# Two mixture-of-experts layers behind a Fourier transform: another order of the 26 products and other PSUM banks

## The chip, the cores and the metric

The kernel runs on one core of a Trainium2 chip. The metric is the device time of one execution in microseconds (us). The kernel before took 10217.74 us (median of 3 runs, 10211.21 to 10218.54).

## The reference

```python
X = np.fft.fft(np.fft.fft(x, axis=1), axis=2)      # x: 8 x 3072 x 256
x = X.real.reshape(24576, 256)
...                                                 # first layer: each row goes to the best one of 8 experts
logits = x @ w_gate;  P = np.exp(logits - logits.max())
for _ in range(8):                                  # Sinkhorn balancing
    P /= P.sum(1, keepdims=True) + 1e-09
    P /= P.sum(0, keepdims=True) + 1e-09
    P *= N / E
for e in range(8):                                  # second layer: every row through every expert
    h = np.maximum(x @ w1[e], 0.0)                  # 256 -> 1024
    out += P[:, e:e + 1] * (h @ w2[e])              # 1024 -> 256
```

All is float32. The change lies in the second layer.

## The kernel before

The first 1850 us hold the transform, the routing and the first layer. The second layer (class `Second`, line 778) fills the rest. It takes the 24576 rows in 24 blocks of 1024, and each block through the 8 experts: 192 rounds, a round being one block `b` and one expert `e`.

In a round the first matrix product `x @ w1[e]` is not done as 32 block products but by a fast scheme with 26: the rows' and the weights' blocks are added and subtracted beforehand, and sums of the 26 products give the 16 hidden blocks of 128 features by 512 columns. The table `STEPS` (line 722) is that scheme and also its schedule. One entry is one **step**, numbered 0 to 25 here. It holds: the PSUM bank (0 to 3) into which the product goes; 1 if the bank starts a new sum, 0 if the product is added to what stands there; the signs of the weight blocks; the sums of row blocks to be formed; which row block is used; a list of operations; and the banks that are free for other use at this step.

The operations of a step, in the loop at line 1105:

- `c k`: ACT copies the bank's running sum to an SBUF tile `v` number k (line 1120, named c18 and so on below).
- `a k`: DVE forms tile k from two others or from the bank (-1) and a tile (line 1125; the tile is called `v` where it is kept, `z` where it goes straight into a hidden block).
- `h o`: ACT takes the positive part of hidden block o, rounded to the matmul's type (line 1061).
- `l o`: DVE forms the rest that the rounding lost (line 1067).
- `m o`: TensorE multiplies hidden block o by w2, 12 matmuls into another four banks (line 1032). A last number 1 means that the block of the round before is meant.

A step's own product is 6 matmuls of 256 columns (line 1114), so a round has 26 x 6 + 16 x 12 = 348. TensorE's order is that of the program. The other engines each work through a queue that a scheduler has laid out when the kernel is built. A product into a bank may start only when every operation that reads the bank's sum so far is done, whether the product adds to that sum or starts a new one. So what counts is how long a bank rests between the last product in it and the next.

During a block's rounds e=6 and e=7 the next block's rows are prepared (`prepare`, line 952): in e=6 TensorE transposes them in four groups of four (`pb`), each group in a bank that the current step lists as free (`bank`, line 947; asked for at steps 0, 4, 8, ... , one group at a time, the first free bank of the list), and ACT copies each to `xb`. Then POOL forms the sums `xt` (line 968), ACT casts each of the 26 operands to `xs` (line 490, "cast"), and POOL forms the rest that the cast lost (line 491). Each `xs` has one buffer, so the cast for step m has to wait for step m of round e=7. In block 0 the Sinkhorn balancing runs beside rounds 0 to 4.

Of the kernel before, what the change touches and what calls it, by code (L numbers as in the profile page):

```python
# [525 lines left out]
class First:  # L526
# [99 lines left out]
    def run(self, second):  # L626
# [93 lines left out]


STEPS = [
# [52 lines left out]
]  # L775


class Second:
# [6 lines left out]
    def weights(self, raw, pool):  # L785
# [18 lines left out]
        for e in range(E):  # L804
            yield
            yield
            for pc in range(NP // 2):
                o = pool.tile([128, 2, 2, 2, 128], F32R, name="qo", tag="qo")
                for n in range(2):
                    a = STEPS[2 * pc + n][2]  # L810
                    v = [(c, r1[:, i % 2, :, i // 2, :]) for i, c in enumerate(a) if c]
# [93 lines left out]
    def run(self, ones, r):  # L905
        nc, tc = self.nc, self.tc
        from contextlib import ExitStack
        with ExitStack() as ctx:
            pool = lambda name, bufs, **k: ctx.enter_context(tc.tile_pool(name=name, bufs=bufs, **k))
            one, xp = pool("n1", 1), pool("nx", 1)  # L910
            ring, ring2 = pool("nw", NW), pool("nw2", NW2)
            hp, vp, zp, hsp = pool("nh", 8), pool("nv", 11), pool("nz", 3), pool("ns", 2)
            ph, py = pool("nph", 1, space=PSUM), pool("npy", 1, space=PSUM)
            ctx.enter_context(tc.manual_schedule(engines={mybir.EngineType.PE}))

# [3 lines left out]
            for k in (1, 0):  # L919
                for s in STEPS:  # L920
                    for o in s[5]:
# [30 lines left out]
            def prepare(r, xs, fast):  # L952
                eng = nc.vector if fast else nc.gpsimd
                blk = {}
                for k in range(2):
                    for h in range(2):
# [6 lines left out]
                        if not fast:  # L963
                            yield
                for m, s in enumerate(STEPS):
                    for o, x, y, c in s[3]:
# [82 lines left out]

            outs = [o[1] for k in (1, 0) for s in STEPS for o in s[5] if o[0] == "m" and o[2] == 1 - k]  # L1050
            cnt, firstj = [0] * 4, None
# [32 lines left out]
            def advance(n):  # L1084
                nonlocal ahead
                for _ in range(n - ahead):
                    next(prep, None)
                ahead = max(ahead, n)

            late_x = None  # L1090
            for u, (b, e) in enumerate(rounds):
# [8 lines left out]
                if (b, e) == (0, HELD):  # L1100
# [3 lines left out]
                    accp[0] = pool("na", 1)  # L1104
                for m, (bk, new, _, _, _, ops, idle) in enumerate(STEPS):
                    if b == e == 0:
# [37 lines left out]
                    if e == 0 and b > 0:  # L1144
                        advance(8 + min(NP, int((m + 24) / 1.5) + 1))
            for s in STEPS:
                for o in s[5]:
# [70 lines left out]
```

## Time and profile before

| | |
|---|---|
| median of 3 runs | 10217.74 us |
| the profiled execution | 10225.79 us |
| its span, first to last instruction | 10224.0 us |
| mean granted TensorE clock | 0.976 |
| busy: PE, DVE, ACT, POOL | 96%, 66%, 44%, 19% |
| second layer: first product, last matmul starts | 1856.1 us, 10211.4 us |

In the profile PE is TensorE's matmuls and PEld its weight loads; DVE, ACT, POOL and SP are the other engines. The end of a matmul in a row is modelled and overlaps the next one's start, so waits of TensorE are read from starts. In steady work matmuls of 256 columns start 0.12 us apart.

### The profile page before, as it was taken

The numbers are of one execution on the slowest core, as the hardware profiler recorded it, in microseconds if no ns is written. First come the engines' busy times: TensorE is split into PE (matmuls) and PEld (weight loads), VectorE is DVE, ScalarE is ACT, GpSimd is POOL, SyncE is SP. The second block draws the span as 40 slices with busy tenths as digits, with TensorE's granted clock in tenths as the row PEclk, the third lists the DMA queues.
The fourth block names the chain that finished last, engine by engine and source line by source line (L and its number), as shares of the span: only waits on it lengthen the run. The fifth ranks groups of instructions, "written<-read, shape, count | busy, mean of one in ns | idle before, by whom it ended". The sixth has DMA issues, their size and how long they took to land.

```text
span 10224.0 us, 194490 instructions
## 1 busy us (share of the span) xinstructions
PE 9811.1 (96%) x77965; PEld 9595.7 (94%) x77965; DVE 6748.1 (66%) x11890; ACT 4457.2 (44%) x8467; POOL 1975.3 (19%) x1866
## 2 busy tenths in 40 slices
PE   7689999899999999999999999999999999999999
PEld 7568898899999999999999999999999999999999
DVE  3357776676666666666666666666666666666666
ACT  3344444444444444444444444444444444444443
POOL 2355555010111011101110111011011101110110
PEclk7789999999999999999999999999999999999999
DMA  4346665566666666666666666666666666666665
GB/s 135 88 162 221 217 227 193 185 228 216 208 214 213 216 212 214 215 212 213 211 210 215 215 214 215 211 215 212 216 209 210 214 216 209 216 215 211 215 207 183
DMA packets 662091, 2102.95 MB, mean 206 GB/s; under 512 B 129057, under 2 KB 185538, under 8 KB 639138
## 3 DMA queue, kind: packets, MB, share of 16 engines
q1 hardware_dynamic: 634992, 2038.02, 61.4%
q0 software_dynamic: 25632, 52.25, 1.6%
q8 instruction: 621, 10.17, 0.4%
q14 instruction: 284, 2.33, 0.1%
q10 hardware_dynamic: 562, 0.18, 0.0%
HBM read 1929.48 MB, written 160.68 MB: 204 GB/s over the span
## 4 chain that ended last, share of the span: by engine, by line
PE 61%; DVE 10%; issue 5%; POOL 3%; ACT 3%; ACTq 0%; DMA 0%; POOLq 0%; DVEq 0%
PE py L1032 32%; PE ph L1114 28%; DVE z L1125 5%; DVE hl L1067 3%; ACT hh L1061 2%; POOL xt L968 2%; POOL xs L491 2%; DVE v L1125 1%; ACT xs L490 1%; ACT v L1120 0%; PE pb L959 0%; POOL out L1010 0%; DVE P L882 0%; DVE acc L987 0%; DVE S L875 0%
## 5 line engine op out<-in xcount | busy, mean ns | idle before, releaser
L1032 PE MATMUL py<-w,hh 128*128 128x256 f32 x24576 | 4579.4, 284 | 0.0
L1114 PE MATMUL ph<-xs,w 128*128 128x256 f32 x29952 | 4145.5, 285 | 177.3 <-DVE z L1125 170.5
L1114 PEld LDWEIGHTS ph<-xs,w 128*128 128x128 f32 x29952 | 3837.2, 193 | 212.4 <-issue 134.1
L1032 PEld LDWEIGHTS py<-w,hh 128*128 128x128 f32 x24576 | 3856.8, 193 | 0.0
L1032 PE MATMUL py<-w,hl 128*128 128x256 f32 x12288 | 3487.6, 284 | 0.0
L1120 ACT COPY v<-ph 128x512 f32<-128x512 f32 x2880 | 1683.3, 585 | 2330.4 <-PE ph L1114 2239.4
L1067 DVE SCALAR_TENSOR_TENSOR hl<-z,hh 128x512 fp32r<-128x512 f32 x2880 | 1974.5, 712 | 878.0 <-ACT hh L1061 850.9
L1061 ACT ACTIVATE hh<-z 128x512 fp32r<-128x512 f32 x2880 | 1747.5, 631 | 1763.7 <-DVE z L1125 1752.6
L1032 PEld LDWEIGHTS py<-w,hl 128*128 128x128 f32 x12288 | 2371.6, 193 | 0.0
L968 POOL TENSOR_TENSOR xt<-xb 128x256 f32<-128x256 f32 x161 | 147.3, 915 | 6281.0 <-ACT xb L961 5928.5
L1125 DVE TENSOR_TENSOR v<-ph,v 128x512 f32<-128x512 f32 x960 | 658.3, 686 | 575.4 <-PE ph L1114 560.1
L1125 DVE TENSOR_TENSOR z<-v,ph 128x512 f32<-128x512 f32 x1152 | 767.2, 680 | 255.7 <-PE ph L1114 254.3
L1006 DVE SCALAR_TENSOR_TENSOR acc<-py,P,acc 128x256 f32<-128x256 f32 x1304 | 570.9, 480 | 404.5 <-PE py L1032 376.7
L1125 DVE TENSOR_TENSOR z<-v 128x512 f32<-128x512 f32 x960 | 695.0, 724 | 103.5 <-ACT v L1120 85.4
L1125 DVE TENSOR_TENSOR z<-ph,v 128x512 f32<-128x512 f32 x768 | 510.0, 684 | 129.6 <-PE ph L1114 129.6
L653 PE MATMUL py<-w2h,hh 128*128 128x264 f32 x1600 | 457.9, 286 | 0.0
L654 PE MATMUL py<-w2l,hh 128*128 128x264 f32 x1600 | 453.2, 283 | 0.0
L655 PE MATMUL py<-w2h,hl 128*128 128x264 f32 x1600 | 453.1, 283 | 0.0
L520 DVE SCALAR_TENSOR_TENSOR hl<-ph,hh 128x512 fp32r<-128x512 f32 x400 | 271.5, 688 | 258.4 <-ACT hh L519 252.2
L1125 DVE TENSOR_TENSOR v<-v 128x512 f32<-128x512 f32 x384 | 280.9, 732 | 243.2 <-ACT v L1120 243.0
L491 POOL TENSOR_TENSOR xs<-xt,xs 128x256 fp32r<-128x256 f32 x437 | 353.2, 814 | 224.8 <-ACT xs L490 224.8
L519 ACT ACTIVATE hh<-ph 128x512 fp32r<-128x512 f32 x400 | 237.8, 599 | 308.8 <-PE ph L514 306.8
(200 smaller groups left out, 7530.1 us busy)
## 6 DMA issues: line engine op xcount, KB each, us to landing
w<-wqd SPq DMA_DIRECT2D x2496, 512.0 KB
w<-w2qd SPq DMA_DIRECT2D x768, 512.0 KB
r<-m1w SPq DMA_DIRECT2D x100, 1024.0 KB
wqd<-qo SPq DMA_DIRECT2D x104, 512.0 KB
x<-y SPq DMA_DIRECT2D x50, 512.0 KB
xs<-zt SPq DMA_DIRECT2D x64, 384.0 KB
rows<-x SPq DMA_DIRECT2D x24, 1024.0 KB
xt<-x SPq DMA_DIRECT2D x31, 768.0 KB
```

What stands on the lines that cost most here:

```text
L491: eng_lo.tensor_tensor(lo, x, hi.bitcast(F32), op=ALU.subtract)
L653: nc.tensor.matmul(p, hh, w2h[:, s], start=(c == 0), stop=False)
L654: nc.tensor.matmul(p, hh, w2l[:, s], start=False, stop=False)
L655: nc.tensor.matmul(p, hl, w2h[:, s], start=False, stop=(c == 7))
L968: eng.tensor_tensor(t, blk[x], blk[y], op=ALU.add if c > 0 else ALU.subtract)
L1006: nc.vector.scalar_tensor_tensor(acc[:, q, :], y[:, q % 2, :], pe(q), acc[:, q, :], op0=ALU.mult, op1=ALU.add)
L1032: nc.tensor.matmul(y[:, q, :], a[:, c], w[:, s, v, :], start=n == k == 0, stop=n == 3 and s == 1 and a is hl, skip_group_check=True)
L1061: nc.scalar.activation(hh, src, AF.Relu)
L1067: nc.vector.scalar_tensor_tensor(hl, src, 0.0, hh.bitcast(F32), op0=ALU.max, op1=ALU.subtract)
L1114: nc.tensor.matmul(p[:, s * 256:(s + 1) * 256], w[:, a, s, :], x[m][:, c, :], start=bool(new) and s == n == 0, stop=n == 2, skip_group_che ...
L1120: nc.scalar.copy(t, p)
L1125: nc.vector.tensor_tensor(t, p if i0 < 0 else v[i0], p if i1 < 0 else v[i1], op=ALU.add if op == "+" else ALU.subtract)
```

## The change

The 26 products come in another order (with other signs and combinations to match), they use other banks, and the tile pool `nz` has four buffers in place of three. The copies c18, c30 and c32 are gone and c17 is new, so that a round has 13 copies in place of 15: a62 and a39 now read the bank itself where they read c18 and c30, and a40 reads c17 where it read c32. Two of the 26 entries, and the pool:

```diff
 STEPS = [
+    (3, 1, (0, 0, 0, 0, 1, 0, 0, 0), (), 1,
+     (('c', 21), ('l', 7, 1), ('m', 0, 1)), (1, 0)),
...
-    (3, 0, (-1, 0, 0, 0, 0, 0, 0, 0), ((1, 10, 8, -1),), 9,
-     (('l', 10, 0), ('a', 53, -1, 35, '-', 0), ('h', 3, 53), ('l', 3, 0), ('a', 54, -1, 41, '-', 0), ('h', 7, 54)), (3, 2, 1, 0)),
+    (1, 0, (-1, 0, 0, 0, 0, 0, 0, 0), ((0, 10, 9, -1),), 8,
+     (('l', 10, 0), ('a', 53, -1, 35, '-', 0), ('h', 3, 53), ('l', 3, 0), ('a', 54, -1, 41, '-', 0), ('h', 7, 54)), (1, 0, 2)),
 ]
...
-            hp, vp, zp, hsp = pool("nh", 8), pool("nv", 11), pool("nz", 3), pool("ns", 2)
+            hp, vp, zp, hsp = pool("nh", 8), pool("nv", 11), pool("nz", 4), pool("ns", 2)
```

What the two tables say of banks and of the w2 products (`m`), by step:

```
step            0  1  2  3  4  5  6  7  8  9 10 11 12 13 14 15 16 17 18 19 20 21 22 23 24 25
bank before     1  3  0  2  1  2  0  1  0  2  1  2  3  1  3  2  3  0  2  1  0  2  1  3  2  3
m before       12  0  1  -  6 10  -  3  7  9  -  -  - 13  -  5  - 15 11  -  4  8  -  2 14  -
bank now        3  2  0  1  3  0  1  3  2  3  2  1  3  2  0  3  1  3  3  2  0  3  2  1  0  1
m now           0  1  6  - 10  3  -  7  9  - 13  -  -  5  -  - 15 11  -  4  8  2  - 14 12  -
```

In the last steps the operations are the same before and now: a43, a50 read the bank at step 22, a58 at step 23, a51 and a52 at step 24, a53 and a54 at step 25. The free banks asked for at steps 0, 4, 8, 12, 16, 20, 24 are before 2, 0, 1, none, none, 0, 2 and now 1, none, none, 1, none, 0, 0; so the four groups of transposes stand behind steps 0, 4, 8 and 20 before and behind 0, 12, 20 and 24 now.

First place: ACT at the start of a plain round (a round without preparation), before, from h6 of the round before to h13. The number behind `ph_` names a sum, which may grow by later products.

```order
L1061 ACTIVATE hh_56680<-z_56678 128x512
L1120 COPY v_56729<-ph_56722 128x512
L1061 ACTIVATE hh_56688<-z_56686 128x512
L1061 ACTIVATE hh_56712<-z_56710 128x512
L1061 ACTIVATE hh_56718<-z_56716 128x512
L1120 COPY v_56752<-ph_56745 128x512
L1120 COPY v_56777<-ph_56770 128x512
L1120 COPY v_56800<-ph_56793 128x512
L1120 COPY v_56814<-ph_56722 128x512
L1061 ACTIVATE hh_56804<-z_56802 128x512
```

Here the copies c18, c15, c7, c21 and c32 of steps 0 to 4 stand one after the other but for h10, h3, h7. The same place now, again from h6 on:

```order
L1061 ACTIVATE hh_56436<-z_56434 128x512
L1120 COPY v_56485<-ph_56478 128x512
L1061 ACTIVATE hh_56444<-z_56442 128x512
L1061 ACTIVATE hh_56468<-z_56466 128x512
L1061 ACTIVATE hh_56474<-z_56472 128x512
L1120 COPY v_56510<-ph_56503 128x512
L1120 COPY v_56535<-ph_56528 128x512
L1061 ACTIVATE hh_56558<-z_56556 128x512
L1120 COPY v_56597<-ph_56590 128x512
L1120 COPY v_56631<-ph_56478 128x512
```

The copies of steps 3 and 4 are gone; the hidden blocks h10, h3 and h7 stand behind the copy of step 0 in both.

Second place: ACT in a round e=7, around steps 14 to 18, before (c37, cast 14, c26, casts 15 and 16, c28, h4, h8, cast 17, h2):

```order
L1120 COPY v_58723<-ph_58418 128x512
L490 CAST xs_58878<-xt_58876 128x256
L1120 COPY v_58738<-ph_58657 128x512
L490 CAST xs_58917<-xt_58915 128x256
L490 CAST xs_58949<-xt_58947 128x256
L1120 COPY v_58782<-ph_58584 128x512
L1061 ACTIVATE hh_58765<-z_58763 128x512
L1061 ACTIVATE hh_58771<-z_58769 128x512
L490 CAST xs_59009<-xt_59007 128x256
L1061 ACTIVATE hh_58812<-ph_58657 128x512
```

Here c28 copies step 17's sum right behind cast 16, ahead of h4 and h8. The same place now (c28, cast 14, c23, casts 15 and 16, h4, h8, c26, cast 17, h2):

```order
L1120 COPY v_58461<-ph_58260 128x512
L490 CAST xs_58657<-xt_58655 128x256
L1120 COPY v_58477<-ph_58470 128x512
L490 CAST xs_58686<-xb_57826 128x256
L490 CAST xs_58744<-xt_58742 128x256
L1061 ACTIVATE hh_58490<-z_58488 128x512
L1061 ACTIVATE hh_58496<-z_58494 128x512
L1120 COPY v_58522<-ph_58470 128x512
L490 CAST xs_58780<-xt_58778 128x256
L1061 ACTIVATE hh_58551<-ph_58470 128x512
```

The copy of step 17's sum has moved behind h4 and h8, and sum 58470 is read by c23 (step 15), c26 (step 17) and h2 (step 18), one bank with steps 17 and 18 in a row.

POOL's queue changes too. At the end of a preparation, from the operand sum of step 23 on, its order before is xt23, rest 23, xt24, xt24, rest 24, xt25, rest 25; now it is xt23, rests 19 to 23, xt24, xt24, xt25, rest 24, rest 25.

## Rows read from the trace of the kernel before

**Rows 1.** The page: busy share, and granted clock in 40 slices (tenths).

```profile
PE 9811.1 (96%) x77965; PEld 9595.7 (94%) x77965; DVE 6748.1 (66%) x11890; ACT 4457.2 (44%) x8467; POOL 1975.3 (19%) x1866
...
PEclk7789999999999999999999999999999999999999
```

**Rows 2.** Waits, 2600 to 9600 us: total us, times, longest us.

```profile
PE ph L1114 <- DVE z L1125: 139.8, 161, 4.9
PEld ph L1114 <- issue: 101.7, 20, 5.1
```

**Rows 3.** Timeline of PE, 2606 to 2632 us: start, us, operation, [idle before <-releaser].

```profile
2606.03 3.04 PE L1114 MATMUL ph<-xs,w 128*128 128x256 f32 x24
2608.91 0.40 PE L1032 MATMUL py<-w,hh 128*128 128x256 f32 x2
...
2631.11 0.28 PE L1032 MATMUL py<-w,hl 128*128 128x256 f32 x1
2631.57 0.95 PE L1114 MATMUL ph<-xs,w 128*128 128x256 f32 x6 [0.18 <-DVE z L1125]
```

**Rows 4.** The chain of waits: start, us, what (steps 10 to 13 of a round).

```profile
2513.17 2.88 PE ph L1114 x24
2606.19 2.88 PE ph L1114 x24
...
2817.01 2.88 PE ph L1114 x24
2860.07 2.88 PE ph L1114 x24
2952.15 2.88 PE ph L1114 x24
```

**Rows 5.** Timeline of DVE, same round boundary (a53 and a54).

```profile
2630.14 1.28 DVE L1125 TENSOR_TENSOR z<-ph,v 128x512 f32<-128x512 f32 x2
```

**Rows 6.** Timeline of PE at a block's start.

```profile
2924.77 0.28 PE L1032 MATMUL py<-w,hl 128*128 128x256 f32 x1
2925.94 1.69 PE L1114 MATMUL ph<-xs,w 128*128 128x256 f32 x12 [0.89 <-DVE z L1125]
...
2928.79 0.28 PE L1032 MATMUL py<-w,hl 128*128 128x256 f32 x1
2933.98 1.62 PE L1114 MATMUL ph<-xs,w 128*128 128x256 f32 x6 [4.91 <-DVE z L1125]
```

**Rows 7.** Timeline of ACT there (casts 23, 24, 25).

```profile
2926.21 0.41 ACT L490 CAST xs<-xt 128x256 fp32r<-128x256 f32 x1 [2.25 <-POOL xt L968]
...
2929.75 0.41 ACT L490 CAST xs<-xt 128x256 fp32r<-128x256 f32 x1 [2.08 <-POOL xt L968]
...
2932.11 0.41 ACT L490 CAST xs<-xt 128x256 fp32r<-128x256 f32 x1 [1.43 <-POOL xt L968]
```

**Rows 8.** Timeline of DVE there (a53 and a54).

```profile
2932.55 1.27 DVE L1125 TENSOR_TENSOR z<-ph,v 128x512 f32<-128x512 f32 x2
```

**Rows 9.** Windows: us, busy PE (x), PEld, DVE, ACT, POOL, then clock, DMA share, GB/s.

```profile
2934.00:2937.50 3.50, 3.50 (x18) 3.50 (x19) 1.63 (x3) 1.16 (x3) 0.00 (x0) 0.56 0.22 61
...
1957.00:1965.00 8.00, 6.52 (x55) 6.34 (x54) 7.75 (x18) 4.63 (x9) 0.00 (x0) 1.00 0.65 216
```

**Rows 10.** Timeline of PE in e=7 (steps 16, 17) and e=6 (step 24).

```profile
2909.77 1.60 PE L1114 MATMUL ph<-xs,w 128*128 128x256 f32 x12
2911.21 0.40 PE L1032 MATMUL py<-w,hh 128*128 128x256 f32 x2
...
2880.50 0.88 PE L1114 MATMUL ph<-xs,w 128*128 128x256 f32 x6
2881.22 0.40 PE L1032 MATMUL py<-w,hh 128*128 128x256 f32 x2
```

**Rows 11.** Timeline of ACT in e=7 (casts 15, 16; c28).

```profile
2912.56 0.71 ACT L490 CAST xs<-xt 128x256 fp32r<-128x256 f32 x2 [3.16 <-POOL xt L968]
2913.18 0.58 ACT L1120 COPY v<-ph 128x512 f32<-128x512 f32 x1
```

**Rows 12.** Timeline of DVE in e=6 (a52).

```profile
2882.47 0.69 DVE L1125 TENSOR_TENSOR v<-ph,v 128x512 f32<-128x512 f32 x1
```

**Rows 13.** Groups by line: count, busy, mean ns, idle before.

```profile
L1061 ACT ACTIVATE hh<-z 128x512 fp32r<-128x512 f32 x2425 | 1470.1, 631 | 1467.2 <-DVE z L1125 1458.0 <-ACT hh L1061 0.8 <-ACT xs L490 0.3
L1120 ACT COPY v<-ph 128x512 f32<-128x512 f32 x2424 | 1416.8, 585 | 1985.0 <-PE ph L1114 1911.4 <-PE py L1032 12.6
...
L968 POOL TENSOR_TENSOR xt<-xb,xt 128x256 f32<-128x256 f32 x180 | 165.9, 922 | 14.1
```

**Rows 14.** Timeline of POOL, first operand sums of a preparation.

```profile
2876.39 0.74 POOL L968 TENSOR_TENSOR xt<-xb 128x256 f32<-128x256 f32 x1 [16.81 <-ACT xb L961]
```

**Rows 15.** Timeline of PE in block 0: a round's step 1, and block 1's coming.

```profile
1957.14 0.28 PE L1032 MATMUL py<-w,hl 128*128 128x256 f32 x1
1958.90 0.95 PE L1114 MATMUL ph<-xs,w 128*128 128x256 f32 x6 [1.48 <-DVE z L1125]
...
2190.55 0.76 PE L1114 MATMUL ph<-xs,w 128*128 128x256 f32 x2 [3.81 <-DVE z L1125]
```

92 rows, old and new, of the table STEPS are left out of this document.

## The prediction

> **What bounds the kernel now.** I read the page first. PE is busy 96% of the span, no other engine over 66%, and the clock stands at full from the fourth slice on [rows 1]. So only TensorE's waits can be gained, and nearly all of the second layer is plain matmul time. The list of waits names them: in 7000 us PE waits 161 times for a DVE result `z` at line 1125 before a first-product matmul, 4.9 us at the longest, and 20 times about 5.1 us behind something without a name [rows 2].
>
> Next the timeline of PE gives the size. A run of 24 matmuls takes 2.88 us from start to start, 0.12 each [rows 3], so a round of 348 has a floor of 41.76 us. In the chain of waits the same four steps of a round come back 210.82 us after five rounds (2606.19 to 2817.01), which is 42.16 a round: 0.40 lost in each [rows 4]. The place is step 1: the last matmul before it starts at 2631.11, its first at 2631.57, 0.34 late, and the six of the step take 0.95 in place of 0.88 [rows 3, 10]. Step 1 writes bank 3; step 25 was the last to write it; and its readers a53 and a54 end at 2631.42, 0.15 before PE goes on [rows 5]. The bank rests for only step 0 and its w2 product, 6 + 12 matmuls, 2.16 us.
>
> The round e=6 shows no loss: 2817.01 to 2860.07 is 43.06, which is 41.76 and three groups of transposes at 0.43. From there to the same steps of the next block's first round it is 92.08 us, and 93.02 one block earlier (2513.17 to 2606.19), against 2 x 41.76 + 0.43 = 83.95 [rows 4]. That is 8.1 and 9.1 lost, 8.6 in the mean, at each of 23 block starts. It falls on step 25 of e=7 (2924.77 to 2925.94, 1.05 over the usual 0.12, waiting for a58 in bank 3) and above all on step 1 of e=0 (2928.79 to 2933.98, 5.07 over) [rows 6]; then the clock is down, 0.56 in the next 3.5 us [rows 9]. What makes bank 3 late here is ACT's queue: casts 23, 24 and 25 each stand 1.4 to 2.3 us waiting for POOL's operand sum [rows 7], behind them stand the hidden blocks, DVE waits for those in order, and a54 ends only at 2933.82 [rows 8].
>
> **The change, part by part.** *The round boundary.* Now a53 and a54 read bank 1, which is next written at step 3, after steps 0, 1, 2 with their w2 products: 3 x 2.16 = 6.48 us of rest in place of 2.16. a51 and a52 (bank 0) are needed at step 2, 6.48 as well; a43 and a50 (bank 2) at step 1, 7.20. In a plain round a54 ends 2.35 us after step 25's last slot (2631.42 against 2631.23 - 2.16), so all 0.40 goes, and what would be late next has 4 us to spare. Of the other banks I took the rest from the two tables: most are 2.88 us and more. Three have 2.16 (steps 8, 15) or 1.44 (step 17), all read by one ACT copy.
>
> *Steps 17 and 18 in a row in bank 3.* Between them lie only the 12 matmuls of m11, 1.44 us. The copy c26 needs about 0.16 to the matmul's end, 0.04 to start (both as ACT follows PE elsewhere), 0.585 [rows 13] and 0.15 until PE goes on [rows 3, 5], together 0.94. h4 and h8 stand ahead of it on ACT. Their inputs a44 and a49 are done 0.16 + 0.04 + 1.28 [rows 5] = 1.48 us after step 16's slots; if both h (2 x 0.63) came only then, c26 would start at 2.74, end at 3.33 and let PE go at 3.48, and step 18 is due at 1.44 + 0.72 + 1.44 = 3.60. With h4 running beside a49 the margin is 0.5. I take no wait in a plain round, with bounds of 0 and 0.4.
>
> A page of the Trainium skill speaks against this place: Perfetto Trace Analysis, section Matmuls, says that independent groups should rotate through different PSUM banks so that one's evacuation overlaps the next group's matmuls. Nine of the 26 steps now go to bank 3, two of them back to back. By that rule the round would wait there for the whole evacuation; the trace has w2 products into other banks to cover it, so by the row it would not. No run yet shows which.
>
> *Step 18 in round e=7.* There the casts stand ahead of c26. Before, casts 15 and 16 waited until 2912.56 for POOL, and c28 behind them ended at 2913.76 [rows 11], 2.55 us after step 17's last slot at 2911.21 [rows 10]. PE did not mind, for bank 0 rested 4.32 us. Now the same delay meets 1.44: 2.55 + 0.15 - 1.44 = 1.26 of wait. h4 and h8 now stand ahead of the copy as well, 2 x 0.63 more [rows 13], 2.5. If POOL is in time it is 0; if POOL is later by the three or four operand sums it used to do before the round (below), 4 or more. I take 1.9, near the rows; ends 0 and 4.
>
> *The transposes in e=6.* They now go behind step 0 into bank 1, where a54 has just read: the same 0.40 as in the plain round before. Behind step 12 into bank 1, read by c46 one step before (0.72 us against 0.94): 0.2. Behind step 24 into bank 0, which a51 and a52 read at that very step: before, a52 ended at 2883.16, 1.94 after the step's slots at 2881.22 [rows 10, 12], the w2 product covers 1.44, and with 0.15 the wait is 0.65. Behind step 20 nothing. Together 1.25 in each of 23 blocks, ends 0.4 and 2.
>
> *The block's start.* The readers' rest grows by 4.32, so of the 5.07 about 0.75 would stay if a54 were as late as before. POOL's tail is shorter by one rest and one cast between casts 23 and 25 (about 0.9 + 0.4), because the three sums for 24 and 25 now stand together. On the other side the fourth transposed group comes behind step 24 instead of step 20, so that POOL's first sums, at 2876.39 before [rows 14], 7 us ahead of the round, start only with it. POOL had idle time in the round (its casts were late), so I expect it to catch up and count 0 here. Then the clock does not fall either: waits of 1.64 us in block 0 are followed by full clock, 1.00 [rows 9, 15].
>
> *The rest.* Two ACT copies fewer in a round, 192 x 2 x 0.585 = 225 us of ACT, but ACT waits for PE most of the time [rows 13], so it is worth nothing by itself; it is the cover if ACT gets tight. The fourth `z` buffer: DVE has the hidden blocks ahead of a53 in its queue anyway, nothing. The first layer prepares the weights by the same table with as many additions; 0, within 3 us either way.
>
> **The sum**, against the profiled execution of 10225.79:
>
> - five plain rounds, 23 blocks: 23 x 5 x 0.40 = 46
> - block starts: 23 x 8.6 = 198
> - block 0 and the last block: four waits of 1.64 at step 1 (1957.14 to 1958.90 is one [rows 15]), one of nearly 4 at 2190.55 [rows 15], three of 0.40: 12
> - new: 23 x (1.9 + 1.25) = -72
>
> That is 184 us less: 10042. The profiled execution ran 8 us over the median of 10217.74, so the forecast against the median is 10034.
>
> **The rivals.** *Nothing new waits* (POOL in time, the transposes covered): 72 less, 9962. For it: fewer ACT operations. Against it: a52's own row gives 0.65 at step 24 whatever POOL does. Chance 0.10.
>
> *The stall at the block's start stays.* POOL loses its head start (four sums, 3.6 us at 0.92 [rows 13]) and does not catch up: then 0.75 + 3.6 - 1.3 = 3 us at step 3 of e=0, and with a clock that falls as before (about 2 us) 5 us, 23 times: 70 to 115 more, 10104 to 10149. For it: ACT's casts were POOL-bound to the last one [rows 7]. Against it: POOL idled between them. Chance 0.16.
>
> *Slower than before: step 18 waits in every round.* If the copy c26 comes behind h8 late in plain rounds too, as the skill's rule on banks would have it, the price of e=7, 1.9 us, is paid in the 169 other rounds as well: 321 more, 10355. It decides from 184 / 169 = 1.1 us a round on. Against it: DVE and ACT are nowhere near full in plain rounds, and h4's and h8's inputs come in 1.48 us. Chance 0.03.
>
> *Nothing changes*, because PE's waits only move to another bank with the same total: would need 8 us of new waits in a block, 10218. Chance 0.02.
>
> **How the numbers follow.** The forecast has 0.69, with its own range of 9990 to 10085 (new waits of 1 to 5.3 us a block). 9960 to 10125 takes in the first rival and half of the second. What a measurement of this kernel can tell from no change is about 0.2%, 20 us. Faster by more: 0.95 (forecast, first and second rival); the same 0.02; slower 0.03.
>
> **What would show it.** Right: plain rounds 41.76 apart; no clock fall at block starts; e=7 with one wait at step 18 of 1 to 3 us, released by an ACT copy; e=6 with short waits before the transposes behind steps 0 and 24. Wrong: a wait in step 18 of plain rounds; a wait over 2 us in e=0; casts that wait for POOL past the end of e=7 by as much as before.

## The result, and the profile after

The changed kernel took 10058.65 us (median of 4 runs, 10057.62 to 10059.45), the kernel before in the same comparison 10214.47 (4 runs, 10206.91 to 10218.54): a ratio of 0.9848, 95% interval 0.9831 to 0.9865. The forecast was 10034 in a range of 9960 to 10125. The profiled execution's span is 10057.7 us in place of 10224.0.

The page after: busy time, share of the span and instructions of each engine, and the clock in 40 slices.

```profile
PE 9761.8 (97%) x77965; PEld 9553.4 (95%) x77965; DVE 6746.0 (67%) x11874; ACT 4330.5 (43%) x8083; POOL 1989.2 (20%) x1866
...
PEclk7789999999999999999999999999999999999999
```

This looks like [rows 1]: as many matmuls, PE one point busier. The ACT copies that went show in its count (8083 in place of 8467) and nowhere in the time. What changed is in the list of waits of the same 7000 us (total us, times, longest us):

```profile
PEld ph L1114 <- ACT v L1120: 38.2, 36, 1.4
PE ph L1114 <- ACT v L1120: 30.9, 36, 1.2
...
PE pb L959 <- DVE v L1125: 9.5, 20, 0.5
PEld pb L959 <- DVE v L1125: 5.8, 20, 0.3
PE pb L959 <- DVE z L1125: 4.9, 20, 0.2
PEld pb L959 <- ACT v L1120: 3.3, 20, 0.2
```

The 161 waits for `z` and the 20 of 5.1 us [rows 2] are gone. What is left waits for copies (36 times, at most 1.4 us: 20 at step 18 of e=7 and 16 at step 10 of e=0) and, in the transposes `pb`, for less. The chain of waits, the same 12 matmuls in successive plain rounds (start, us, what):

```profile
2605.31 1.44 PE ph L1114 x12
...
2647.07 1.44 PE ph L1114 x12
...
2688.83 1.44 PE ph L1114 x12
```

They stand 41.76 us apart, which is the floor itself, against 42.16 before [rows 4]. The start of a block on PE, from step 25 of e=7 to step 2 of e=0:

```profile
2914.43 1.60 PE L1114 MATMUL ph<-xs,w 128*128 128x256 f32 x12
...
2917.30 0.88 PE L1114 MATMUL ph<-xs,w 128*128 128x256 f32 x6
...
2919.47 0.88 PE L1114 MATMUL ph<-xs,w 128*128 128x256 f32 x6
```

No wait stands there any more [rows 6]: the steps come 2.16 us apart. Casts 24 and 25 on ACT there, then a53 and a54 on DVE:

```profile
2914.30 0.41 ACT L490 CAST xs<-xt 128x256 fp32r<-128x256 f32 x1 [1.31 <-POOL xt L968]
...
2916.05 0.39 ACT L490 CAST xs<-xt 128x256 fp32r<-128x256 f32 x1
```

```profile
2917.94 1.27 DVE L1125 TENSOR_TENSOR z<-ph,v 128x512 f32<-128x512 f32 x2
```

Cast 24 still waits for POOL, cast 25 no longer [rows 7], and a54 ends at 2919.21, 2.4 us before step 3 needs its bank (2921.63) [rows 8]. So the clock does not fall [rows 9] (windows: us, busy time of five engines, clock, DMA share, GB/s):

```profile
2914.00:2917.50 3.50, 3.50 (x31) 3.50 (x31) 3.34 (x5) 1.82 (x4) 3.01 (x4) 1.00 0.55 160
2917.50:2921.00 3.50, 3.50 (x31) 3.50 (x30) 3.50 (x7) 2.87 (x5) 0.00 (x0) 1.00 0.85 284
```

The new wait is where it was forecast, at step 18 of e=7. PE, then ACT there:

```profile
2898.60 0.88 PE L1114 MATMUL ph<-xs,w 128*128 128x256 f32 x6
2899.32 0.40 PE L1032 MATMUL py<-w,hh 128*128 128x256 f32 x2
...
2900.64 0.28 PE L1032 MATMUL py<-w,hl 128*128 128x256 f32 x1
2902.10 1.69 PE L1114 MATMUL ph<-xs,w 128*128 128x256 f32 x12 [1.18 <-ACT v L1120]
```

```profile
2900.11 0.41 ACT L490 CAST xs<-xt 128x256 fp32r<-128x256 f32 x1 [2.45 <-POOL xt L968]
2900.43 1.14 ACT L1061 ACTIVATE hh<-z 128x512 fp32r<-128x512 f32 x2
2901.48 0.57 ACT L1120 COPY v<-ph 128x512 f32<-128x512 f32 x1
```

Cast 16 waits 2.45 us for POOL's sum, h4 and h8 follow, then the copy c26, and 0.05 us after its end PE goes on, 1.34 us late (2902.10 less 2900.64 and 0.12). Before, c28 stood right behind cast 16 [rows 11] and PE did not feel it [rows 10].

### The profile page after: what moved, and what is told of

Its sections match the earlier page's. It is cut to its first block, busy times and chain, and to the rows that moved or that the text cites. A ratio compares the mean times of both kernels' runs of the same rounds, so it can differ in the third digit from the quotient of the medians.

```text
span 10057.7 us, 195266 instructions
## 1 busy us (share of the span) xinstructions
PE 9761.8 (97%) x77965; PEld 9553.4 (95%) x77965; DVE 6746.0 (67%) x11874; ACT 4330.5 (43%) x8083; POOL 1989.2 (20%) x1866
## 4 chain that ended last, share of the span: by engine, by line
PE 69%; DVE 4%; issue 4%; POOL 2%; ACT 2%; DMA 0%; POOLq 0%; ACTq 0%; DVEq 0%; SPq 0%
PE py L1032 38%; PE ph L1114 31%; DVE z L1125 2%; POOL xs L491 1%; DVE v L1125 1%; ACT hh L1061 1%; DVE hl L1067 1%; POOL xt L968 1%; PE pb L959 1%; ACT v L1120 0%; ACT xs L490 0%; DMA hs<-hdd 0%; DVE P L882 0%; DVE S L875 0%; POOL out L1010 0%
## 5 line engine op out<-in xcount | busy, mean ns | idle before, releaser
L1120 ACT COPY v<-ph 128x512 f32<-128x512 f32 x2496 | 1463.6, 587 | 1966.6 <-PE ph L1114 1807.7
L968 POOL TENSOR_TENSOR xt<-xb 128x256 f32<-128x256 f32 x161 | 127.0, 795 | 6433.4 <-ACT xb L961 6426.2
L1125 DVE TENSOR_TENSOR z<-v,ph 128x512 f32<-128x512 f32 x1344 | 898.5, 681 | 481.5 <-PE ph L1114 481.4
L1125 DVE TENSOR_TENSOR z<-v 128x512 f32<-128x512 f32 x768 | 547.1, 732 | 6.7
L514 PE MATMUL ph<-xh,w1h 128*128 128x512 f32 x800 | 319.7, 400 | 15.3 <-DVE hl L520 14.6
```

The source lines that it names most:

```text
L514: nc.tensor.matmul(p, w[:, k * 1024 + c * 128:k * 1024 + (c + 1) * 128], x[:, k, :], start=(i == 0), stop=(i == 5))
L1120: nc.scalar.copy(t, p)
L1125: nc.vector.tensor_tensor(t, p if i0 < 0 else v[i0], p if i1 < 0 else v[i1], op=ALU.add if op == "+" else ALU.subtract)
```

## The experiments

Three of the chips used run the part ahead of the second layer some 210 us faster than the chip of the first comparison (first product at 1641 to 1650 us in place of 1856 before and 1858 after), and the kernel before then takes 10007 to 10008 us in all. So the ratios are compared, and the length of the second layer, first product to last matmul: 8355.28 before, 8187.49 after. Round lengths are the mean over blocks 1 to 22, from the start of step 0 to the next. A wait of PE is the distance of two starts less 0.12; it too is given as the mean of these blocks where no single row is named.

**a_again: the changed kernel on another chip.** No edit.

> The changed kernel once more, on the chip of this call, as the base for the runs beside it. Its second layer should again take 8187 us from the first product to the last matmul, with 1.4 us at step 18 of e=7 and 0.4 and 0.6 us before the transposes behind steps 0 and 24 of e=6; the ratio to the kernel before 0.983 to 0.985.

Measured: 9839.70 us, ratio 0.9831 (0.9816 to 0.9846), second layer 8176.70. Rounds e=0 to 5 take 41.76 each, e=6 45.08, e=7 43.19. On the first chip e=0 took 42.27; this round's loss (below) is that chip's. The rest repeats, and the rival that the stall at the block's start stays is out: e=0 has no wait.

**b_rot: the order of before, with only the banks rotated from round to round.**

```diff
+ROT = ((0, 1, 2, 3), (2, 0, 3, 1), (3, 2, 1, 0), (1, 3, 0, 2))
...
                 for m, (bk, new, _, _, _, ops, idle) in enumerate(STEPS):
+                    bk, idle = ROT[u % 4][bk], tuple(ROT[u % 4][i] for i in idle)
```

> The order of before, its 15 copies, its pool of three z buffers and its POOL queue; only the banks change names from round to round (period 4), so that the bank of steps 23 and 25 is next written at step 3 and not at step 1. Theory of the forecast (what costs is the rest of the bank that a53 and a54 read): the 0.40 us in plain rounds goes, the 5.07 us at the block's start falls to about 0.75 and the clock stays up; the 1.05 us at step 25 of e=7 stays, and the first group of transposes in e=6 now waits 0.40. Per block 10.6 - 0.75 - 1.15 - 0.4 = 8.3 less, 23 times 190, and some 8 in block 0: about 10015 us, that is a little faster than the changed kernel, since step 18 has no wait here. Rival (the gain at the block's start comes from fewer ACT copies and POOL's other order): only the plain rounds gain, 23 x 2.0: about 10165 us.

Measured: 9804.93 us, ratio 0.9797 (0.9782 to 0.9812), second layer 8151.09. Plain rounds 41.76, e=0 42.63, e=6 43.86, e=7 42.91. Its waits in 7000 us ahead of first-product matmuls that name a reader of a sum:

```profile
PE ph L1118 <- DVE z L1129: 30.9, 40, 0.9
PEld ph L1118 <- DVE z L1129: 22.0, 20, 1.1
```

The 161 waits have become 40, idle for at most 0.9 us: by the starts 1.06 at step 25 of e=7, as before, and 0.81 at step 3 of e=0, where 0.75 was expected. Longer rest across the round boundary is thus worth the whole gain by itself; the new order of the products is not needed for it, and costs 25 us of it again (8176.70 against 8151.09): e=6, e=7 and block 0 are longer by 1.22, 0.28 and 14 us, e=0 and the last block shorter by 0.87 and 2.3.

**a_swap: the new order, with the rest at the round boundary taken away** (banks 1 and 2 exchanged in every second round, so that step 1 writes the bank that step 25 left).

```diff
+ROT = ((0, 1, 2, 3), (0, 2, 1, 3))
...
+                    bk, idle = ROT[u % 2][bk], tuple(ROT[u % 2][i] for i in idle)
```

> The changed kernel with banks 1 and 2 exchanged in every other round, so that the bank that a53 and a54 read at step 25 is again written at step 1 of the next round. Theory of the forecast: plain rounds wait 0.40 us at step 1 again; at the block's start a54 ends about 2.06 us after step 1 is due in the changed kernel's trace, so 2.1 us of wait there (5.07 before), with no fall of the clock. Per block 2.0 + 0.4 + 2.1 = 4.5 more, 23 times 103: about 10160 us. Rival (copies, z buffer and POOL's order are the cause): 10058 us as the changed kernel.

Measured: 9977.03 us, ratio 0.9969 (0.9957 to 0.9981), second layer 8316.31. Plain rounds take 42.23 again, e=0 44.83; step 1 of e=0 waits 2.06 in every block, as expected. The waits of PE, and the windows just behind that wait in blocks 1 and 2:

```profile
PE ph L1118 <- DVE z L1129: 75.0, 143, 1.9
PEld ph L1118 <- issue: 41.4, 20, 2.1
```

```profile
2032.00:2035.00 3.00, 2.83 (x24) 2.86 (x25) 3.00 (x8) 1.34 (x3) 0.50 (x1) 1.00 0.37 89
...
2375.00:2378.00 3.00, 2.13 (x10) 2.16 (x11) 3.00 (x7) 2.00 (x4) 0.00 (x0) 0.66 0.06 25
```

140 us are lost again by this alone (8316.31 against 8176.70), of the 179 that lie between 8176.70 and the 8355.28 of before. Expected were 103 and no fall of the clock. It fell, as in the second window, in 15 of the 23 rounds e=0, which take 45.37, and not in the other 8, which take 43.88: 15 x 1.49 = 22 us of the 140. The wait is 2.06 and not the 5.07 of before, since DVE's end of the round comes about 3 us earlier in the new order (4.06 after step 0's start in place of 7.1).

**a_nz3: the new kernel with three `z` buffers.**

```diff
-            hp, vp, zp, hsp = pool("nh", 8), pool("nv", 11), pool("nz", 4), pool("ns", 2)
+            hp, vp, zp, hsp = pool("nh", 8), pool("nv", 11), pool("nz", 3), pool("ns", 2)
```

> The changed kernel with three z buffers in place of four. Theory of the forecast: DVE has the hidden blocks ahead of a53 in its queue anyway, so no change, 10058 us within 10. Rival (the fourth buffer lets DVE run ahead at the round's end): 0.3 us or more in each of 192 rounds, 10115 us or more.

Measured: 9833.76 us, ratio 0.9826 (0.9811 to 0.9841), second layer 8176.40 against 8176.70. The buffer is worth nothing.

**a_idle: only the lists of free banks in another order**, each time the bank first that has rested longest (steps 0, 10, 11, 21 to 25).

```diff
-     (('c', 21), ('l', 7, 1), ('m', 0, 1)), (1, 0)),
+     (('c', 21), ('l', 7, 1), ('m', 0, 1)), (0, 1)),
...
-     (('c', 46),), (1, 2)),
+     (('c', 46),), (2, 1)),
...
```

> The changed kernel, with the lists of free banks put in the order of how long each has rested (step 0: 0 then 1; step 11: 2 then 1; step 24: 2, 3, 0; and five more), so that transposes and the Sinkhorn sums take the bank that was read longest ago. Theory (a transposed group waits for the last reader of the bank that it was given): the waits behind steps 0 and 24 of e=6, 0.41 and 0.64 us in the trace, go, 23 x 1.05 = 24 us; in block 0 the Sinkhorn sums behind step 24 lose their 2.1 to 3.2 us and most of the 0.84 behind step 11, some 12 us with the clock: about 10022 us. Rival (DVE and ACT are late as such, and the wait moves to the next product or sum): 10050 us or more.

Measured: 9793.92 us, ratio 0.9786 (0.9773 to 0.9799), second layer 8131.93; a second time, as **a_idle_2** on a further chip, 9792.02 us, 0.9784 (0.9771 to 0.9797), 8130.03.

> The kernel of a_idle once more, beside a_xt16 on one chip, so that their times can be compared directly. By theory A of a_xt16 it is 30 to 40 us slower than a_xt16, by rival B 5 to 20 us. If the wait at step 10 of round e=0 belongs to the chip, both show it or neither; if it belongs to the kernels after and a_early, only a_xt16 can show it.

Round e=6 falls from 45.08 to 43.97, and block 0 from 379.81 (a_again) to 359.86. The column sum of the balancing (line 889) borrows such a bank too. Its group (count, busy and mean ns, PE idle ahead of it) in before, after and a_idle:

```profile
L889 PE MATMUL pb<-cs,ones 128*128 128x8 f32 x16 | 3.0, 259 | 5.7 <-DVE z L1125 5.7
```

```profile
L889 PE MATMUL pb<-cs,ones 128*128 128x8 f32 x16 | 3.0, 259 | 11.6 <-DVE v L1125 8.9 <-ACT v L1120 2.7
```

```profile
L889 PE MATMUL pb<-cs,ones 128*128 128x8 f32 x16 | 2.3, 213 | 0.0
```

After, it stood behind step 24 in bank 0, which a52 reads at that very step as the last in DVE's queue. PE's and DVE's rows for the first of these, in the kernel after:

```profile
1913.75 0.36 PE L889 MATMUL pb<-cs,ones 128*128 128x8 f32 x2 [3.06 <-DVE v L1125]
1913.96 2.08 PE L1114 MATMUL ph<-xs,w 128*128 128x256 f32 x12
```

```profile
1912.92 0.68 DVE L1125 TENSOR_TENSOR v<-ph,v 128x512 f32<-128x512 f32 x1
```

a52 ends at 1913.60, PE goes on at 1913.75, and the next 12 matmuls take 2.08 us where 12 take 1.60 at full clock.

**a_noxt: POOL's 20 row-block sums left out**, so that the output is another; the casts read the rows' blocks themselves.

```diff
+                        if not fast:
+                            blk[8 + o] = blk[x]
+                            continue
```

> The changed kernel; left out are POOL's 20 sums of row blocks in the preparation of blocks 1 to 23 (the casts take a plain row block instead). Theory of the forecast (casts 15 and 16 wait for POOL's sums, and h4, h8 and c26 wait behind them on ACT): the 1.4 us at step 18 of e=7 goes, e=7 takes 41.8 us in place of 43.2, 23 x 1.4 = 32 us less than the changed kernel; the waits in e=6 stay as they are. Rival (c26 is late by h4 and h8 and the casts' own time on ACT, whatever POOL does): 0.7 us or more stays at step 18.

Measured: 9807.04 us, ratio 0.98 (0.9785 to 0.9815), second layer 8142.97. Round e=7 takes 41.76, as short as a plain round; the wait at step 18 is gone whole. Its cause is POOL's sums, and h4 and h8 ahead of the copy cost nothing when cast 16 is in time. (What waits remain on PE are the transposes'.)

**a_c26dve: a_idle with the copy c26 on DVE.**

```diff
-                            nc.scalar.copy(t, p)
+                            (nc.vector.tensor_copy if o[1] == 26 else nc.scalar.copy)(t, p)
```

> The kernel with the free banks reordered (a_idle), and the one copy c26 done by DVE in place of ACT. Theory (ACT's queue behind the casts makes c26 late): DVE is not behind the casts; after l15, l11, a44 and a49 it can copy 0.7 us after step 17, and the 1.36 us at step 18 of e=7 falls under 0.4: 23 x 1.0 = 23 us less than a_idle. DVE takes 0.69 us more in each round of 28, which plain rounds hide. Rival (DVE waits in order for l4 and l8, whose h4 and h8 stand behind the casts too): 1 us or more stays, no gain over a_idle.

Measured: 9847.95 us, ratio 0.9842 (0.9827 to 0.9857), second layer 8184.58, e=7 45.31. The wait for it, 20 blocks:

```profile
PEld ph L1114 <- DVE v L1120: 51.2, 20, 2.6
```

It grows from 1.33 to 2.52, and behind it the clock falls in 14 of blocks 1 to 22. In DVE's queue the copy stands behind l4 and l8, which wait for h4 and h8, which ACT makes only behind cast 16. The queue was changed, not what stands ahead.

**a_sw18: a_idle with steps 18 and 19 exchanged**, so that bank 3 rests 2.16 us in between in place of 1.44.

```diff
-    (3, 0, (0, 1, 0, 0, 0, 0, 0, 0), ((4, 6, 11, -1),), 12,
...
-    (2, 0, (0, 1, 0, 0, 0, 0, 1, -1), ((3, 0, 2, -1), (4, 9, 11, 1)), 12,
+    (2, 0, (0, 1, 0, 0, 0, 0, 1, -1), ((5, 6, 11, -1), (3, 0, 2, -1), (4, 9, 11, 1)), 12,
...
+    (3, 0, (0, 1, 0, 0, 0, 0, 0, 0), (), 13,
...
```

> The kernel with the free banks reordered (a_idle), and steps 18 and 19 exchanged, so that bank 3 rests 2.16 us and not 1.44 after step 17, with m4 behind the second of them and one more slot for a row-block sum. Theory (step 18 waits 1.36 us because c26 meets 1.44 us of rest): 0.72 more rest leaves 0.64 at most, 23 x 0.7 = 17 us less than a_idle, plain rounds at 41.76. Rival (a57 and a56 come earlier on DVE and wait for c26 themselves, or bank 3 after its h2, l2 and a42 is late at step 21): as slow as a_idle or slower, with a wait of 0.3 us or more at step 21 in plain rounds.

Measured: 9858.67 us, ratio 0.9848 (0.9835 to 0.9862), second layer 8198.15, slower than a_idle. The wait for c26 shrinks to 0.62 as it should, but a42 on DVE now comes a step later and holds up step 21 of e=7 and the transposes of e=6:

```profile
PE ph L1114 <- DVE v L1125: 33.2, 20, 1.7
PE pb L959 <- DVE v L1125: 29.3, 20, 1.5
PE ph L1114 <- ACT v L1120: 9.3, 20, 0.5
```

**a_early: a_idle with the transposes of e=6 behind steps 0, 3, 7 and 11**, so that POOL can start earlier.

```diff
-                    if e == 6 and b + 1 < NB and m % 4 == 0:
-                        advance(m // 4 + 1)
+                    if e == 6 and b + 1 < NB and m in (0, 3, 7, 11):
+                        advance((0, 3, 7, 11).index(m) + 1)
...
```

> The kernel of a_idle with one thing moved: the four groups of transposes of round e=6 come behind steps 0, 3, 7 and 11 in place of 0, 12, 20 and 24, so that POOL's operand sums may begin some 20 us earlier. Theory A (POOL is late at cast 16 because its first sums start too late): the waits of e=6 at steps 12 and 20 (0.14 + 0.26) go, 23 x 0.40 = 9 us, and step 18 of e=7 falls from 1.36 to 0.5 or less, 23 x 0.9 to 23 x 1.36 = 21 to 31 us; second layer 8092 to 8102 against 8131.9. Rival B (each cast m has to wait for step m of e=7 anyway, POOL idles between and is late at cast 16 whatever its start): step 18 keeps 1.0 us or more, only the 9 us go, second layer 8115 to 8125. Rival C (the new places collide with a bank just read, or ACT's four copies and early casts delay the copies of e=6): new waits of 0.3 us or more in e=6 or e=7, second layer 8130 or more.

Measured, on the chip of the first comparison: 10007.5 us against 10216.76, ratio 0.9797 (0.9784 to 0.9811), second layer 8138.18. Without the 0.62 us by which e=0 is longer there (22 blocks, 13.6 us) that is 8125, where rival B had it. Step 18 still waits 1.35; in e=6 one wait of 0.18 at step 13 takes the place of those behind steps 12 and 20. POOL, from its fifth sum to the first rest, and around the sum for cast 16:

```profile
2477.77 1.56 POOL L968 TENSOR_TENSOR xt<-xb,xt 128x256 f32<-128x256 f32 x2
2500.26 1.29 POOL L491 TENSOR_TENSOR xs<-xb,xs 128x256 fp32r<-128x256 f32 x1 [20.93 <-ACT xs L490]
...
2520.91 1.88 POOL L491 TENSOR_TENSOR xs<-xb,xs 128x256 fp32r<-128x256 f32 x2
2522.76 1.89 POOL L491 TENSOR_TENSOR xs<-xt,xs 128x256 fp32r<-128x256 f32 x2
2524.72 0.73 POOL L968 TENSOR_TENSOR xt<-xb 128x256 f32<-128x256 f32 x1
```

The head start ends in 20.93 us of waiting for cast 0, which waits for step 0 of e=7. From there on nothing is earlier than in the kernel after: there this sum starts at 2899.35 and step 18 at 2902.10, here at 2524.72 and 2527.47, the sum 2.75 us ahead of the step in both. The sum stands in POOL's queue behind four rests.

**a_xt16: a_early with that one sum (row blocks 0 and 1, for the operand of step 16) moved among POOL's first**, in a buffer of its own.

```diff
-    (0, 1, (0, 0, 0, 0, 0, 0, -1, 0), ((1, 5, 7, 1), (2, 3, 9, 1), (3, 1, 10, 1)), 11,
+    (0, 1, (0, 0, 0, 0, 0, 0, -1, 0), ((1, 5, 7, 1), (2, 3, 9, 1), (3, 1, 10, 1), (5, 0, 1, -1)), 11,
...
-    (1, 1, (0, 0, 1, -1, 0, 0, 0, 0), ((2, 0, 1, -1),), 10,
+    (1, 1, (0, 0, 1, -1, 0, 0, 0, 0), (), 13,
...
```

> The kernel of a_early with one thing moved: POOL's sum for the operand of step 16 gets a buffer of its own and is formed among the first sums, in the 20 us in which POOL has nothing to do, in place of behind four rests in round e=7. POOL's and ACT's queues are otherwise the same. Theory A (cast 16 is late because its sum stands in POOL's queue behind four rests, and that alone holds up c26): cast 16 no longer waits, the wait at step 18 falls from 1.38 us to 0.3 or less in 23 blocks, 25 to 32 us, round e=7 takes 42.1 or less, second layer (without what step 10 of e=0 loses on one of the chips) 8093 to 8100 against 8125. Rival B (POOL's work as a whole is late, and another operand's cast or h4 and h8 hold c26 up): 0.6 us or more stays at step 18 or comes back at a later step of e=7, e=7 takes 42.5 or more, second layer 8108 or more.

Measured: 9753.72 us, ratio 0.9746 (0.9733 to 0.9759), second layer 8091.92. It beats all the others; a_idle_2 beside it took 9792.02. ACT and PE at the same place:

```profile
2321.34 0.42 ACT L490 CAST xs<-xt 128x256 fp32r<-128x256 f32 x1
2322.40 1.23 ACT L1061 ACTIVATE hh<-z 128x512 fp32r<-128x512 f32 x2 [0.64 <-DVE z L1125]
2323.53 0.57 ACT L1120 COPY v<-ph 128x512 f32<-128x512 f32 x1
```

```profile
2324.55 1.60 PE L1114 MATMUL ph<-xs,w 128*128 128x256 f32 x12
```

Cast 16 waits for nothing, c26 ends at 2324.10, and step 18 starts in its turn. Rounds e=0 to 5 and e=7 now all take 41.76; 0.17 at step 13 of e=6 is the one wait left in the mean of blocks 1 to 22.

## Why the prediction was right, and where its sum was off

| term | forecast, us | measured, us |
|---|---|---|
| five plain rounds | -46 | 23 x 5 x 0.41 = -47 |
| block starts (before: e=7 1.61, e=0 7.00 over 41.76) | -198 | 23 x 8.61 = -198 |
| block 0 and the last block (what the other rows leave of the second layer's -167.8) | -12 | -4 |
| step 18 of e=7 (e=7 43.20, less 41.76) | +44 | 23 x 1.44 = +33 |
| transposes in e=6 (45.05, less 41.76 and 4 x 0.43) | +29 | 23 x 1.57 = +36 |
| step 10 of e=0 | not seen | 23 x 0.51 = +12 |
| ahead of the second layer | 0 | +2 |
| sum | -184 | -166, as by the span |

Step 18, put 11 us too dear, hides a part of the 29 that were missed at block 0, the transposes, step 10 and ahead of the second layer; that part is luck. The sum's 10042 stands against the profiled execution's 10059.45, 17 us off. The forecast of 10034 missed the median by 25: it took off 8 more because the profiled execution of before lay 8 over its median, and the one after lies only 0.8 over its own.

*The round boundary* held by its own reasoning: rest, not order, carried it (b_rot), and taking it away undoes most of it (a_swap). That the clock stays up once the wait is gone also held: the windows of the block's start read 1.00. The 0.75 that would stay with an a54 as late as before stood in b_rot (0.81); in the new order it goes as well, since DVE's round ends 3.0 us earlier, where the prediction saw 1.3 in POOL's tail and counted on none of it.

*Steps 17 and 18 in one bank.* No wait in plain rounds, as worked out from rows. The Trainium skill's rule (Perfetto Trace Analysis, Matmuls) that groups should rotate through banks so that evacuation overlaps the next group is met here without a rotation, by the 12 w2 matmuls in between, 41.76 us a round; where the evacuation itself is held up, in e=7, the repeated bank costs 1.34, and there the trace agrees with the rule.

*Step 18 of e=7* had the right mechanism and was 0.5 too dear: cast 16 let ACT go on 1.11 us after step 17's slots (2900.43 less 2899.32), and not 1.97 as before (2913.18 less 2911.21 [rows 10, 11]), and the two h took 1.05 in place of 1.26. a_noxt, a_early and a_xt16 settle the cause: one sum's place in POOL's queue.

*The transposes*: 0.40 behind step 0 (forecast 0.40), 0.12 behind 12 (0.2), 0.64 behind 24 (0.65), but 0.25 behind step 20, which was put at nothing. There the list gives bank 0, which a41 reads at that very step; this reader was overlooked. a_idle takes away 1.04 of these 1.41 by the choice of bank, a_early 0.19 more by the places.

*Block 0* is the step of the sum that failed: "block 0 and the last block ... 12" less. Block 0 was 1.9 us longer than before (379.75 against 377.85) in place of shorter. Its rounds 0 to 5 grew from 277.33 to 280.56, though the waits of 1.64 at step 1 are gone. The prediction followed the products' banks and the transposes' to their new lists, and forgot that the balancing's column sum borrows a bank by the same lists. It met the bank that DVE reads last, four times for 2.1 to 3.2 us. Round e=6 grew from 50.99 to 55.47, by 4.5 where 1.25 was forecast: behind step 24 the transposes now wait for a DVE that in block 0 also adds up rows held back (line 987). DVE and PE there:

```profile
2188.59 1.67 DVE L987 SCALAR_TENSOR_TENSOR acc<-hs,P,acc 128x256 f32<-128x256 f32 x4 [0.83 <-DMA hs<-hdd]
...
2191.61 0.66 PE L959 MATMUL pb<-ident,rows 128*128 128x128 f32 x2 [4.34 <-DVE v L1125]
```

a_idle takes 20 us out of block 0 by the order of those lists alone, 17 of them in rounds 0 to 5.

*Step 10 of e=0* stays open. On the chip of the first comparison, in 16 of the rounds e=0 of after and 19 of a_early, a copy on ACT, a sum on DVE and a weight load on SP start together, 2 to 3 us later behind PE's steps 6 and 7 than in a_again, while PE's starts go on 0.12 apart. ACT, DVE and SP in one such round of after:

```profile
3608.00 0.59 ACT L1120 COPY v<-ph 128x512 f32<-128x512 f32 x1 [3.86 <-PE py L1032]
```

```profile
3607.99 0.69 DVE L1125 TENSOR_TENSOR v<-ph,v 128x512 f32<-128x512 f32 x1 [4.78 <-PE py L1032]
```

```profile
3607.99 0.32 SPq L934 DMA_DIRECT2D w<-wqd  x1
```

The profile names a w2 matmul of PE as what ended the first two waits; the sum reads the bank of step 6, the copy that of step 7, whose first matmuls had started at 3604.29 and 3605.01. Neither a_again nor the other runs on three further chips show it. It goes with that chip and not with the kernel alone; why was not found.

## What to carry to other kernels

Where PE waits a fraction of a microsecond at the same place of each round, count for each accumulator bank the matmuls between its last write and its next, across the end of the loop too, and set against it the readers with all that stands ahead of them in their engine's queue. Everything that borrows a bank has to be in that count, the small helpers (a column sum, a transpose) as well, and should get the bank that has rested longest. If a reader is late behind an operation that waits for another engine, look at the place of that operation's input in the other engine's queue: one sum moved forward was worth 33 us here (8125 to 8091.92), while an earlier start of the whole queue and a change of the reader's engine were worth little or less than nothing.

## What was not expected of the hardware

- The chips differ ahead of the second layer: its first product comes at 1846 to 1858 us on one chip and at 1641 to 1650 on three others, while the second layer is the same within 0.2% (8187.49 and 8176.70 for one kernel). The difference lies in the transform, whose last matmul (line 241) ends at 608.4 us in after and at 397.2 in a_again. The first 500 us of the two, the last three numbers being clock, DMA share and GB/s:

```profile
0.00:500.00 500.00, 368.49 (x2625) 334.30 (x2625) 184.36 (x873) 180.43 (x601) 155.01 (x166) 0.77 0.40 114
```

```profile
0.00:500.00 500.00, 470.59 (x3542) 411.39 (x3543) 301.17 (x1376) 256.87 (x796) 253.65 (x248) 0.92 0.58 173
```

  What holds the slower chip up there was not found.
- Shortening a wait does not always spare the clock, and the same wait does not always cost it: behind the 2.06 us of a_swap it fell in 15 of 23 blocks (0.66 in 3 us of one of them) and stayed at 1.00 in 8. Behind the 5.07 us of before it fell in all 23 ([rows 9] show one), behind a_sw18's 1.82 in none.
